# An attention and mixture-of-experts kernel: when one read is asked for, which engine squares 13 tiles, and where one counting and one router product stand

## The chip, the cores and the metric

The kernel runs on one core of a Trainium2 chip. The metric is the device time of one execution in microseconds; the time of a kernel is the median of its runs. The engines are called by their usual names: TensorE (PE in the profile; PEld is its weight load), VectorE (DVE), ScalarE (ACT), GpSimd (POOL) and SyncE (SP), which issues most of the DMAs.

## What is computed

Eight batches of 1856 tokens go through an attention without softmax; its output, token by token, goes through 16 experts in 4 groups, one expert for each token.

```python
scores = z @ z.T / S                  # z: 8 x 1856 x 64
out = u * (maximum(scores, 0)**2 @ v) # u, v: 8 x 1856 x 256
g = argmax(x @ w_group)               # x: the 14848 rows of out
e = argmax(x @ w_expert[g])
y[token] = softmax_g * softmax_e * (maximum(x @ w1[g, e], 0) @ w2[g, e])   # F = 1024
```

All is float32. The kernel splits each factor of a product into a high part and a low part and adds two or three products.

## The kernel before

**Attention.** A batch has 1856 queries, cut into four quarters (chunks) c = 0 to 3 of 512, 512, 512 and 320 columns in batches 1 to 7 (the last quarter is the one of 320), and 512, 512, 416, 416 in batch 0. Each quarter runs over 15 key tiles of 128 keys; one (batch, quarter, key tile) is a step s, and its place in the quarter is i. The order of the key tiles in a quarter stands in `KORD`. The main loop runs over the steps: `scores(s + 6)` prepares a step six ahead, `attn_v(s)` adds its products with v to the two banks o of the quarter.

**A native tile.** `scores` makes two score products into one of three score banks (lines 438 and 439), ScalarE reads the bank with Relu into r (L442), squares it, and from the square come a high part ah and a low part al. Two ways: ScalarE squares r in place (L450), VectorE copies it into ah (L451) and subtracts (L455, or L458 for the last key tile); or, in the tiles that `ACT_TWICE` lists by quarter, ScalarE squares twice, once into ah (L447) and once in place (L448), and VectorE only subtracts.

**A mirrored tile.** The score matrix is symmetric, so in batches 1 to 7 the tiles below the diagonal aren't computed again. VectorE transposes a tile in 32 x 32 blocks (st, mt), SP writes it to DRAM (sym), and later reads it back (at, `load_mirror`); ScalarE copies at into ah (L427), VectorE subtracts (L428). In the first three quarters the block on the diagonal is halved too: of its four key tiles the first two are transposed (dt), written by one DMA (dg, L362), and read back by four DMAs into dl (`load_diag`, L372); for the third and the fourth key tile only the right half is computed, and ScalarE copies the left half from dl (L466), VectorE subtracts (L467). `DGL` says how many steps before its first user the read is asked for, counted in `scores`.

**The end of a quarter.** `chunk_end` multiplies o by u into xT (VectorE, L508). Some steps later, by `defer`: xh (ScalarE, L514) and xl (VectorE, L519), `logits` (four router products pl, lines 561 and 562), `logits_out` (a copy lgp by ScalarE, L569, and a transposing DMA into lgx), and `planes` (copies by ScalarE, L543, and transposing DMAs that put the rows in order, L549). `LG` is the number of steps from the end of the quarter to `logits`; `logits_out` follows one step later, the planes begin at LG + 2 except in the third quarter.

**Routing.** `route(b, half, hs)` takes two quarters' logits (one, in the last half of batch 7), picks the expert in small VectorE operations, and counts: three products pk (L684 to L686) give each token its place in its expert's bucket, VectorE adds them to the running `base` (L700), and POOL scatters the rows to DRAM (L721). It is a generator, and the main loop takes two of its pieces in each step (three to five in batch 7). Before pk it yields a number: so many steps pass. pl and pk use the same single bank, ps_m.

**What sets the order.** From step 15 to the last quarter the order of TensorE, ScalarE and VectorE is the order of the code. The order on SP and POOL is made by a planner, which takes what the code emits first among what its own timing says is ready. Tiles r, ah, al, z, mt, dt and dl share 27 slots.

**Experts.** At the end of batch 6 the experts are sorted by their counts so far, the first expert's weights (raw_e) are loaded in batch 7 (its ScalarE copies are L204 and L197), and from about 773 us on all time goes to the experts' products.

Of the kernel before, what the change touches and what calls it, by code (L numbers as in the profile page):

```python
# [29 lines left out]
def tile_glu_attn_moe(  # L30
# [12 lines left out]
    B, D, S = uT.shape  # L43
# [7 lines left out]
    NK = NKF + 1  # L51
# [18 lines left out]
    HT = 64  # L70
    NST = 2
    NQT = 27
    ACT_TWICE = ((1, 7, 8, 10, 9, 11), (5, 9, 12), (), ())
    HALF = 256
    DGL = 4
    KT = 4
    MC = 4
    KB = [0, 1, 2, 3]
# [44 lines left out]
    def bank(pl, tag, name):  # L123
        return pl.tile([P, 512], F32, tag=tag, name=name)
# [94 lines left out]
    def defer(step, fn):  # L219
        deferred.append((step, fn))  # L220
# [154 lines left out]
    def load_mirror(b, c, cc):  # L375

        if cc < NQ - 1:
            at = new_at(f"at_{b}_{c}_{cc}").rearrange("p (g x) -> p g x", x=2 * P)
            src = sym.pop((b, c, cc)).rearrange("(g r) (j x) -> j r g x", r=32, x=2 * P)
            for j in range(4):  # L380
                nc.sync.dma_start(at[j * 32:(j + 1) * 32], src[j])
            ats[(b, c, cc)] = at.rearrange("p g (h t x) -> p t h g x", h=2, t=KT)
            return
        g = QW[b][cc] // 32
        at = new_at(f"at_{b}_{c}_{cc}").rearrange("p (g x) -> p g x", x=P)
        src = sym.pop((b, c, cc))[0:g * 32, :].rearrange("(g r) (j x) -> j r g x", r=32, x=P)
        for j in range(4):
            nc.sync.dma_start(at[j * 32:(j + 1) * 32, 0:g, :], src[j])
        ats[(b, c, cc)] = at[:, 0:g, :].rearrange("p g (t x) -> p t g x", t=KT)
# [9 lines left out]
    def key(b, c, i):  # L399
        if (b, c) == (B - 1, NQ - 1):  # L400
            return (0, 1, 12, 2, 3, 14, 4, 5, 13, 6, 7, 8, 9, 10, 11)[i]
        return KORD[c][i] if MB[0] <= b < MB[1] else i

    NS = len(steps)
# [4 lines left out]
    def scores(s):  # L409
# [3 lines left out]
        for far in (ATL, 12):  # L413
            lb, lc, li = steps[min(s + far, NS - 1)]
            lk = key(lb, lc, li)
            if lk % KT == 0 and mirrored(lb, lc, lk) and ((lc, lk) == (3, 8) and lb < B - 1) == (far != ATL):
                load_mirror(lb, lk // KT, KB[lc])
        lb, lc, li = steps[min(s + DGL, NS - 1)]
        lk = key(lb, lc, li)
# [25 lines left out]
        mirror = MB[0] <= b < MB[1] and KB[c] < MC and k // KT < MC and c < POS[k // KT]  # L445
        if k in (ACT_TWICE[c] if MB[0] <= b < MB[1] else ()) and s >= NK:
            held(nc.scalar.activation(out=ah, in_=a, func=AF.Square))  # L447
# [50 lines left out]
    def chunk_end(s):  # L498
        b, c, k = steps[s]
# [16 lines left out]
        def rest_x():  # L516
            xh, xl = xhl
            for d in range(ND):
                nc.vector.tensor_sub(out=xl[:, d, 0:w], in0=xT[:, d, :], in1=f32(xh[:, d, 0:w]))  # L519
# [18 lines left out]
        def planes(d):  # L538

            for t0, t1, q in ((0, w // P, P), (w // P, nt, part)):  # L540
                if t1 > t0:
                    src = xT[:, d, t0 * P:t0 * P + (t1 - t0) * q].bitcast(U16)
                    nc.scalar.copy(  # L543
                        out=pl[:, t0:t1, 2 * d:2 * d + 2, 0:q],
                        in_=src.rearrange("p (t q h) -> p t h q", q=q, h=2),
                    )
            if d == ND - 1:
                for t in range(nt):
                    nc.sync.dma_start_transpose(  # L549
                        rows[:, t, 0:D].bitcast(U16).rearrange("p (g d) -> p g d", d=P),  # L550
                        pl[:, t].rearrange("p g q -> p (g q)"),
                    )
# [20 lines left out]
                lgx.rearrange("p t h l -> p (t h) l"), lgp[:, 0:nt].rearrange("p t h q -> p (t h q)")  # L573
            )

        LG = (7 if b == B - 1 and c < 2 else (11 if c == 2 else 8 if c == 0 else 7)) if s + 1 < NS - NK else 2
        XO = 2 if s + 1 < NS - NK else 0
        (split_x() if XO == 0 else defer(s + XO, split_x))
        (rest_x() if XO == 0 else defer(s + XO + 1, rest_x))
        PL = XO + 1 if not XO or c == 2 else LG + 2  # L580
        defer(s + PL, lambda: planes(0))
        defer(s + PL + 1, lambda: planes(1))
        defer(s + LG, logits)
        defer(s + LG + (1 if XO else 0), logits_out)
        wait = 5 if last else 12 if b == 0 and c < 2 else (17 if c == 1 and b < B - 1 else 15) if s + 1 < NS - NK else 8
        alone = b == B - 1 and c >= NQ - 2
        if c % 2 or alone:
            gens.append((max(s + wait, PFILL[-1] + 2), route(b, c // 2, (c % 2,) if alone else (0, 1))))
# [21 lines left out]
    def route(b, half, hs):  # L610
# [65 lines left out]
        if len(hs) > 1:  # L676
            nc.vector.tensor_add(out=pre[:, 4:8], in0=pre[:, 4:8], in1=pre[:, 3:4].to_broadcast([P, 4, NE]))
            yield
        yield {(B - 1, 1, 0): 5, (B - 1, 1, 1): 1, (B - 2, 1, 0): 7, (0, 1, 0): 11}.get((b, half, hs[0]), 9 if half or b == B - 1 else 7)
        pk = bank(ps_m, "m", f"pk_{name}")  # L680
        W = NT8 * NE
        ohf = oh16.rearrange("p i e -> p (i e)")
# [179 lines left out]
    def phase1(name, wt, x, W, between=None, stack=True):  # L862
        xh, xl = x
        hs = []
        for f in range(NF):
            ps = bank(ps_s, "s", f"ph_{name}_{f}") if f % 2 == 0 else bank(ps_o, "o", f"ph_{name}_{f}")
            fs = slice(f * P, (f + 1) * P)
            o = ps[:, 0:W]
            for d in range(ND):
                nc.tensor.matmul(o, wt["l"][d][:, fs], xh[:, d, 0:W], start=(d == 0), stop=False)  # L870
                nc.tensor.matmul(o, wt["h"][d][:, fs], xh[:, d, 0:W], start=False, stop=False)  # L871
                nc.tensor.matmul(o, wt["h"][d][:, fs], xl[:, d, 0:W], start=False, stop=(d == ND - 1))  # L872
            hh = new_z(f"hh_{name}_{f}")
            hl_ = new_z(f"hl_{name}_{f}")
            nc.scalar.activation(out=hh[:, 0:W], in_=o, func=AF.Relu)  # L875
            wf = W - HT if stack and half(W) else W
            los = [(hl_[:, 0:wf], 0, wf)]
            if wf < W:
                los.append((hh[:, W:W + HT], wf, W))
            for dst, c0, c1 in los:  # L880
                nc.vector.scalar_tensor_tensor(out=dst, in0=o[:, c0:c1], scalar=0.0, in1=f32(hh[:, c0:c1]),  # L881
                                               op0=ALU.max, op1=ALU.subtract)
            hs.append((hh, hl_))
            if between:
                between(f)
        return hs
# [148 lines left out]
    for s in range(NS):  # L1035
        b, c, k = steps[s]
# [39 lines left out]
        if k == NK - 1:  # L1076
            chunk_end(s)
# [145 lines left out]
    for i, (e, r0, n) in enumerate(blocks):  # L1223
# [21 lines left out]
        hs = phase1(i, wts[e], x, n, mid, not turned)  # L1245
# [25 lines left out]
    with tc.If(kreg > 0) as _c, tc.For_i(0, kreg) as iv:  # L1271
# [18 lines left out]
        hs = phase1("ov", wt, x, OVT)  # L1290
# [42 lines left out]
```

## Time and profile before

| | us |
|---|---|
| median of 3 runs | 1464.62 (1464.35 to 1467.05) |
| the profiled execution | 1458.71 |
| its span, first to last instruction | 1457.0 |
| VectorE busy, share of the span | 79% |
| ScalarE busy, share of the span | 65% |

TensorE's clock was granted in full over the whole span (0.999 in the mean). The share of busy time is a mean over the attention part, where TensorE, VectorE and ScalarE all have much to do and the DMA engines as well, and the expert part, where TensorE alone is full. A wait is shown as an idle time of an engine and what ended it. The span's start is 0 us in all rows.

### The profile page before, as it was taken

How to read it: one execution, taken by the hardware profiler on the slowest of the kernel's cores; microseconds unless marked ns; L12 is line 12 of the kernel's file. 1: busy time of each engine (PE TensorE's matmuls, PEld its weight loads, DVE VectorE, ACT ScalarE, POOL GpSimd, SP SyncE). 2: the span in 40 equal slices, each digit the busy share in tenths (PEclk: the TensorE clock that was granted, in tenths of full speed). 3: DMA queues.
4: the chain of work that ended last, by engine and by line, in shares of the span. 5: the costliest groups of instructions: out<-in, count | busy, mean ns of one | idle time of the engine just before them, and what ended most of it. 6: DMA issues, size and time to landing. Idle time of an engine off the chain costs nothing. (4 is left out here: it accounts for less than half of the span.)

```text
span 1457.0 us, 22526 instructions
## 1 busy us (share of the span) xinstructions
PE 1434.2 (98%) x7113; PEld 1234.2 (85%) x7113; DVE 1144.1 (79%) x2388; ACT 940.3 (65%) x1690; POOL 322.5 (22%) x405
## 2 busy tenths in 40 slices
PE   9999999999999999999999999999999999999997
PEld 7888788878888888888878999898888888999986
DVE  7888989899998999989988576776565666566664
ACT  8888698797887988878865345444444444444442
POOL 0002033221332223212224222112111211222122
PEclk9999999999999999999999999999999999999999
DMA  9987979969799698997885464455434555555421
GB/s 320 334 220 214 243 176 266 245 188 245 186 271 245 181 244 196 260 241 181 222 215 154 102 168 98 118 131 137 127 82 118 136 125 132 128 138 133 129 61 44
DMA packets 394346, 260.61 MB, mean 179 GB/s; under 512 B 263424, under 2 KB 357508, under 8 KB 394225
## 3 DMA queue, kind: packets, MB, share of 16 engines
q1 hardware_dynamic: 382400, 228.13, 61.5%
q0 software_dynamic: 11744, 30.90, 7.3%
q8 instruction: 56, 0.92, 0.3%
q14 instruction: 66, 0.53, 0.1%
q10 hardware_dynamic: 80, 0.13, 0.0%
HBM read 113.79 MB, written 94.72 MB: 143 GB/s over the span
## 5 line engine op out<-in xcount | busy, mean ns | idle before, releaser
L486 PE MATMUL o<-ah,vl 128*128 128x512 f32 (+2 forms) x960 | 356.7, 372 | 7.0 <-DVE ah L451 4.2
L487 PE MATMUL o<-ah,vh 128*128 128x512 f32 (+2 forms) x960 | 354.6, 370 | 0.0
L489 PE MATMUL o<-al,vh 128*128 128x512 f32 (+2 forms) x896 | 330.6, 370 | 1.0 <-DVE al L428 0.8
L881 DVE SCALAR_TENSOR_TENSOR hl<-ph,hh 128x512 fp32r<-128x512 f32 (+12 forms) x288 | 174.0, 610 | 147.2 <-ACT hh L875 146.6
L944 PE MATMUL yT<-hh,w_e 128*128 128x512 f32 (+12 forms) x1120 | 268.8, 360 | 0.0
L875 ACT ACTIVATE hh<-ph 128x512 fp32r<-128x512 f32 (+12 forms) x288 | 153.6, 536 | 148.6 <-PE ph L872 146.0
L969 POOL DMA_INDIRECT out_dram<-y,meta x126 | 127.2, 1010 | 495.7 <-DVE y L967 476.1
L944 PEld LDWEIGHTS yT<-hh,w_e 128*128 128x128 f32 x1120 | 200.1, 188 | 25.2
L486 PEld LDWEIGHTS o<-ah,vl 128*128 128x128 f32 x960 | 180.2, 188 | 39.6 <-DVE ah L451 6.7
L871 PE MATMUL ph<-xh_m,w1h_e 128*128 128x512 f32 (+12 forms) x576 | 207.2, 360 | 0.0
L870 PE MATMUL ph<-xh_m,w1l_e 128*128 128x512 f32 (+12 forms) x576 | 206.8, 360 | 0.0
L442 ACT ACTIVATE r<-sc 128x512 f32<-128x512 f32 (+3 forms) x312 | 169.1, 542 | 58.3 <-PE sc L439 56.2
L872 PE MATMUL ph<-xl_m,w1h_e 128*128 128x512 f32 (+12 forms) x576 | 203.0, 359 | 0.0
L487 PEld LDWEIGHTS o<-ah,vh 128*128 128x128 f32 x960 | 180.3, 188 | 26.5
L489 PEld LDWEIGHTS o<-al,vh 128*128 128x128 f32 x896 | 168.1, 188 | 29.5 <-DVE al L455 2.3
L455 DVE TENSOR_TENSOR al<-r,ah 128x512 fp32r<-128x512 f32 (+3 forms) x280 | 177.1, 633 | 19.5 <-ACT r L448 2.6
L721 POOL DMA_INDIRECT bucket<-rows,di x121 | 135.1, 1116 | 176.6 <-DVE rows L718 88.4
L944 PE MATMUL yT<-hl,w_e 128*128 128x512 f32 (+12 forms) x560 | 159.1, 360 | 0.0
L947 ACT COPY yp<-yT 128x1024 uint16<-128x1024 uint16 (+2 forms) x70 | 59.3, 848 | 144.4 <-PE yT L944 140.0
L450 ACT ACTIVATE r<-r 128x512 f32<-128x512 f32 (+3 forms) x249 | 142.8, 573 | 7.9
L870 PEld LDWEIGHTS ph<-xh_m,w1l_e 128*128 128x128 f32 x576 | 108.2, 188 | 13.3
L871 PEld LDWEIGHTS ph<-xh_m,w1h_e 128*128 128x128 f32 x576 | 108.2, 188 | 13.0
(170 smaller groups left out, 2097.6 us busy)
## 6 DMA issues: line engine op xcount, KB each, us to landing
raw_e<-in_w_dram SPq DMA_DIRECT2D x64, 512.0 KB
sym<-st SPq DMA_DIRECT2D x42, 512.0 KB
at<-sym SPq DMA_DIRECT2D x84, 256.0 KB
bucket<-padrow SPq DMA_DIRECT2D x32, 660.0 KB
at<-sym SPq DMA_DIRECT2D x84, 160.0 KB
vr<-in_v_dram SPq DMA_DIRECT2D x23, 512.0 KB
ut<-in_uT_dram SPq DMA_DIRECT2D x23, 512.0 KB
sym<-mt SPq DMA_DIRECT2D x42, 256.0 KB
```

Source lines behind the costliest of these rows:

```text
L442: held(nc.scalar.activation(out=a, in_=ps[:, w0:w], func=AF.Relu, scale=1.0 / S))
L450: held(nc.scalar.activation(out=a, in_=a, func=AF.Square))
L455: held(nc.vector.tensor_sub(out=al, in0=a, in1=f32(ah)))
L486: held(nc.tensor.matmul(o, vl[:, dsl], ah, start=(i == 0), stop=False))
L487: held(nc.tensor.matmul(o, vh[:, dsl], ah, start=False, stop=end and al is None))
L489: held(nc.tensor.matmul(o, vh[:, dsl], al, start=False, stop=end))
L870: nc.tensor.matmul(o, wt["l"][d][:, fs], xh[:, d, 0:W], start=(d == 0), stop=False)
L871: nc.tensor.matmul(o, wt["h"][d][:, fs], xh[:, d, 0:W], start=False, stop=False)
L872: nc.tensor.matmul(o, wt["h"][d][:, fs], xl[:, d, 0:W], start=False, stop=(d == ND - 1))
L875: nc.scalar.activation(out=hh[:, 0:W], in_=o, func=AF.Relu)
L881: nc.vector.scalar_tensor_tensor(out=dst, in0=o[:, c0:c1], scalar=0.0, in1=f32(hh[:, c0:c1]), op0=ALU.max, op1=ALU.subtract)
L944: nc.tensor.matmul(o, wt["2"][f // 2][:, w0:w0 + P], hs[f][q // 2][:, 0:n], start=((f, q) == (0, 0)), stop=((f, q) == (NF - 1, 2)))
```

## The change

The change moves work, and neither adds nor removes a product. `DGL` goes from 4 to 7. `ACT_TWICE`, by quarter, goes from six and three key tiles to eight and five. `LG` of batch 7's second quarter (c = 1) goes from 7 to 9; that of its first quarter stays 7. The counting products of `route(0, 0)` come 10 steps after the yield ahead of them, and not 7; those of `route(0, 1)` lose their entry (11) and fall to the 9 of all second halves.

```diff
-    ACT_TWICE = ((1, 7, 8, 10, 9, 11), (5, 9, 12), (), ())
+    ACT_TWICE = ((0, 4, 1, 6, 5, 8, 10, 11), (5, 10, 9, 11, 12), (), ())
...
-    DGL = 4
+    DGL = 7
...
-        LG = (7 if b == B - 1 and c < 2 else (11 if c == 2 else 8 if c == 0 else 7)) if s + 1 < NS - NK else 2
+        LG = (7 + 2 * c if b == B - 1 and c < 2 else (11 if c == 2 else 8 if c == 0 else 7)) if s + 1 < NS - NK else 2
...
-        yield {(B - 1, 1, 0): 5, (B - 1, 1, 1): 1, (B - 2, 1, 0): 7, (0, 1, 0): 11}.get((b, half, hs[0]), 9 if half or b == B - 1 else 7)
+        yield {(B - 1, 1, 0): 5, (B - 1, 1, 1): 1, (B - 2, 1, 0): 7, (0, 0, 0): 10}.get((b, half, hs[0]), 9 if half or b == B - 1 else 7)
```

## Rows read from the trace of the kernel before

**Rows 1.** The page, first part: engine, busy us (share of the span) xinstructions.

```profile
PE 1434.2 (98%) x7113; PEld 1234.2 (85%) x7113; DVE 1144.1 (79%) x2388; ACT 940.3 (65%) x1690; POOL 322.5 (22%) x405
```

**Rows 2.** TensorE's waits, whole span: tile and line <- releaser: total us, times, longest.

```profile
PE o L486 <- DVE ah L451: 4.2, 5, 1.1
PE o L486 <- DVE ah L458: 2.6, 5, 0.5
PE pl L561 <- DVE base L700: 2.2, 1, 2.2
PE pk L684 <- ACT lgp L569: 1.7, 1, 1.7
PE pl L562 <- DVE xl L519: 1.6, 1, 1.6
```

**Rows 3.** Stretches, fourth quarters (batches 1 to 6): length, busy of PE, PEld, DVE, ACT, POOL.

```profile
655.04:675.39 20.35, 18.64 (x114) 16.60 (x113) 19.54 (x46) 18.30 (x36) 6.57 (x9) 1.00 0.65 135
sum 117.53, PE 111.45 PEld 99.69 DVE 113.27 ACT 105.07 POOL 39.32; mean PE 18.57 PEld 16.62 DVE 18.88 ACT 17.51 POOL 6.55
```

**Rows 4.** TensorE in time, batch 6: start, us, line, operation [idle before <-releaser].

```profile
665.29 0.41 PE L486 MATMUL o<-ah,vl 128*128 128x320 f32 x1 [1.12 <-DVE ah L451]
...
666.29 0.31 PE L487 MATMUL o<-ah,vh 128*128 128x320 f32 x1
666.44 0.31 PE L489 MATMUL o<-al,vh 128*128 128x320 f32 x1
```

**Rows 5.** ScalarE's waits, 110 to 770 us; ScalarE in time, third quarters.

```profile
ACT ah L466 <- DMA dl<-dg: 23.0, 16, 3.8
...
182.60 0.41 ACT L466 CAST ah<-dl 128x256 fp32r<-128x256 f32 x1 [2.41 <-DMA dl<-dg]
...
644.23 0.39 ACT L442 ACTIVATE r<-sc 128x256 f32<-128x256 f32 x1 [1.44 <-PE sc L439]
...
647.58 0.41 ACT L466 CAST ah<-dl 128x256 fp32r<-128x256 f32 x1 [2.52 <-DMA dl<-dg]
```

**Rows 6.** VectorE in time, end of batch 6's third quarter and behind it.

```profile
649.66 0.30 DVE L451 CAST ah<-r 128x256 fp32r<-128x256 f32 x1 [1.21 <-ACT r L450]
...
651.85 1.23 DVE L293 TENSOR_TENSOR vl<-vr,vh 128x1024 fp32r<-128x1024 f32 x1 [1.10 <-ACT vh L292]
...
659.32 1.28 DVE L508 TENSOR_TENSOR xT<-o,ut 128x512 f32<-128x512 f32 x2
```

**Rows 7.** SP's DMA issues in time, batch 6's third quarter.

```profile
633.26 4.64 SPq L549 DMA_TRANSPOSE rows<-pl  x3
...
639.58 0.44 SPq L495 DMA_DIRECT2D ut<-in_uT_dram  x1
640.11 0.54 SPq L372 DMA_DIRECT2D dl<-dg  x1
...
641.79 1.63 SPq L372 DMA_DIRECT2D dl<-dg  x3
```

**Rows 8.** SP's waits, 110 to 770 us, at the issue of dl.

```profile
SPq L372 <- DMA dg<-dt: 11.2, 5, 3.3
```

**Rows 9.** ScalarE and TensorE in time, start of batch 6's first quarter.

```profile
576.74 0.63 ACT L447 ACTIVATE ah<-r 128x512 fp32r<-128x512 f32 x1
577.40 0.63 ACT L448 ACTIVATE r<-r 128x512 f32<-128x512 f32 x1
...
578.84 0.59 ACT L442 ACTIVATE r<-sc 128x512 f32<-128x512 f32 x1
...
580.95 0.48 PE L438 MATMUL sc<-zm,z2h 128*128 128x512 f32 x1
```

**Rows 10.** ScalarE in time, batch 7's third quarter.

```profile
741.10 1.00 ACT L569 COPY lgp<-pl 48x1024 uint16<-48x1024 uint16 x1
...
743.03 1.04 ACT L543 COPY pl<-xT 128x1024 uint16<-128x1024 uint16 x1
747.57 1.15 ACT L204 CAST w_e<-raw_e 128x512 fp32r<-128x512 f32 x2 [3.50 <-DMA raw_e<-in_w_dram]
```

## The prediction

> **What bounds the kernel now.** I read the page's first part, then TensorE's waits, then the stretches in which it waits. TensorE is busy 1434.2 us of the 1457.0 us span [rows 1], so no more than 22.8 us can be won without taking products away, and the change takes none away. TensorE's five longest waits for other engines sum to 12.3 us [rows 2], and all are at lines of the attention part. The expert part behind it shows none of that size, so a wait taken out of attention shortens the span one for one, if it doesn't come back later.
>
> The waits are of two kinds. Three stand once each: the first counting product pk waits 1.7 us for the copy lgp (batch 0), a router product pl waits 2.2 us for `base` (batch 1), another waits 1.6 us for xl (batch 7) [rows 2]. The rest, "o waits for ah", stands mostly in the fourth quarter (c = 3) of batches 1 to 6. Six such quarters last 117.53 us together, 20.35 the one of batch 6 [rows 3]. There the first wait is 1.12 us; TensorE's products of 320 columns start 0.15 us apart and are drawn 0.31 us long [rows 4], so an idle time begins 0.16 us behind the moment at which the next product could have started. With that, the quarter's two waits (1.12, and 0.54 for the ah of L458) and the products right behind them, which start about 0.1 us late five times, come to 2.5 us, and the quarter without them to 17.85 us. 117.53 - 6 x 17.85 = 10.4 us is lost in these six.
>
> Why: in the third quarter ScalarE, in order, reaches the copy of the diagonal's transposed quarter (L466) and waits for its read dl: 2.52 us in batch 6, from 645.06 to 647.58 [rows 5]; the six idle times in the third quarters of batches 1 to 6 (the first, 2.41 us, and the last are shown) sum to 10.6 us; ScalarE's waits for dl in all quarters are 23.0 us [rows 5]. VectorE then waits 1.21 us for ScalarE's r and 1.10 us for vh [rows 6], and after that has no gap until the late ah. It reaches xT at 659.32 [rows 6], though TensorE began the fourth quarter at 655.04 [rows 3]. So VectorE enters the fourth quarter 4 us late, and what it is late there TensorE pays. The six waits for dl (10.6) and the six losses (10.4) are nearly the same sum.
>
> **Part 1, the read asked for seven steps ahead.** The order of ScalarE, VectorE and TensorE is fixed by the code, and the read moves on SP's queue alone. In the third quarter it is now emitted at step i = 3, behind the u read of that step; with 7 it is emitted at i = 0, ahead of u but still behind the transposes of rows and the z read (emitted at i = 11 and 12 of the quarter before). In batch 6 SP issues rows from 633.26 to 637.9, then z and two mirror writes, u at 639.58, one dl at 640.11, then v and a mirror write, then three dl from 641.79 [rows 7]. Ahead of u the four stand from 639.58: the first 0.53 us earlier, the other three from 640.1 instead of 641.79, 1.7 us earlier, and they overtake three transfers of 256 to 512 KB besides. Taken at 2.0 us: of the wait of 2.52, 0.5 stays. In the six batches I take min(wait, 2.0): 2.0 + 1.5 + 1.1 + 2.0 + 1.0 + 2.0 = 9.6. VectorE can follow that far, because its gaps just there (1.21 + 1.10) are larger, and it doesn't run into TensorE's end of the quarter, of which it is 4 us late. **Sum -9.6 us.** Bounds: nothing at all (the read lands as late as now) to -10.4. I take the value near the upper end because the issue order, [rows 7], leaves little else to hold it. What is late next: ScalarE's vh, z2h and `at` copies behind it show no wait in that stretch of the trace, so they move up with it. Queued behind the four dl on SP are u, v and the mirror writes, 2 us later at most; ScalarE and VectorE show no wait for u or v anywhere in batches 1 to 6. In the first two quarters nothing is won on TensorE, which doesn't wait there; in the second the dl already stands on SP waiting for its own write to land (11.2 us in 5 waits, [rows 8]), and an earlier issue only makes SP stand longer.
>
> **Part 2, ScalarE squares twice in 13 tiles for 9.** In the first quarter 0, 4, 6, 5 are added and 7, 9 taken out, in the second 10, 11 are added. Each added tile takes a copy (L451; 0.30 us for 256 columns at 649.66 [rows 6], so up to 0.6 for 512) from VectorE and gives ScalarE a second square, 0.66 us from the start of L447 to the start of L448 [rows 9]. TensorE shows no wait for VectorE in these quarters of batches 1 to 6, so that gain is worth nothing there. ScalarE's cost may not: the next score product but two needs a score bank that L442 frees. In batch 6 the product of tile 8 starts at 580.95 and the bank that it takes was freed by tile 6's L442 (578.84 + 0.59 = 579.43): 1.52 us of room [rows 9]. Tiles 0 and 4 stand before it and add 2 x 0.66 = 1.32, which leaves 0.2; the tiles up to 5 have the same order of room. So TensorE waits between 0 (room enough) and 0.66 us (one square on the path) in each of six batches: 0 to +4 us; I take 0.1 each, near the row's room. **Sum +0.6 us.**
> The Trainium skill's "ScalarE: Activation LUTs", section "What ACT_TABLE_LOAD costs", gives an ACTIVATE with immediate operands 186 ns + 0.833 ns an element, with 93 ns of overlap back to back: by estimate 0.52 us for 512. The trace has 0.66. By the page's figure the two squares would leave 0.5 us of room and this part would cost nothing.
>
> **Part 3, the countings.** The first counting (0, 0) comes three steps later, at the last step of batch 0. lgp has long been copied then, so the wait of 1.7 us (1.84 with the pitch) goes. Its VectorE steps and eight scattering DMAs on POOL come three steps later too; the next user of its bank is five steps behind. The counting (0, 1) loses its entry and comes after 9 steps, not 11: `base` two steps earlier, five and not three steps before the router product that waits 2.2 us (2.39) for it. VectorE is that much ahead of TensorE or the scores themselves would wait. What is late next is xl for the same product, emitted between, so I leave 0.5. **Sum -1.8 - 1.9 = -3.7 us.** Bounds: -4.2, and 0 if VectorE's lag turns up as waits in batch 1.
>
> **Part 4, the router product of batch 7's second quarter two steps later.** The wait for xl (1.6, with pitch 1.76) goes. But lgp, the planes and their transposes move by two steps too, and that puts them behind a wait: lgp (741.10, 1.00 us) and the first planes copy (743.03, 1.04 us) now run while ScalarE has nothing better, before it waits 3.50 us for the weights until 747.57 [rows 10]. Moved, these 2.04 us come behind 747.57, among tiles that TensorE needs at once. So about what is won is paid back in the fourth quarter: between -1.8 and +2. **Sum 0.**
>
> **Sum.** -9.6 + 0.6 - 3.7 + 0 = -12.7. The profiled execution took 1458.71 us (span 1457.0) and would take 1446.0. The median of the runs, 1464.62, stands 5.9 above it; nothing here explains the difference, so I carry it: 1464.62 - 12.7 = 1451.9.
>
> **Rivals.**
> (a) The read lands no earlier, as the DMA engines and not SP's order set its landing, or VectorE's own load in the fourth quarter takes the place of the wait. For it: the last dl is issued by 643.4 and its user starts at 647.58 [rows 5, 7], so 4 us of the way are in the engines. Against: what it now waits behind there is just what it would overtake. Then of part 1 no more survives than what the first dl gains, 0.53, in six batches: 0 to -3.2, taken as -2, and the time is 1464.62 - 2 + 0.6 - 3.7 = 1459.5.
> (b) Hardly any gain: ScalarE becomes the bound at the start of the first quarter. If the whole square (0.66) stands on the path twice in each of six batches, +7.9, and 1464.62 - 9.6 + 7.9 - 3.7 = 1459.2; with half of part 1 failing as well, 1464.0.
> (c) Slower: SP blocks. If the planner puts the early read ahead of the row transposes and the z read, SP must stand until dg has landed. From 633.26 that could be up to 639.6: dg is issued just before 633.26 and dl at 640.11 went without a wait, so the write landed by then. z is then read up to 6 us later, and ScalarE, which already waits for z there, has 1.44 us of waiting for scores and the 2.52 us for dl [rows 5] to give; 6 - 4 = 2 us of lateness stay and go to the fourth quarter, on top of its loss. 6 x 2 + 0.6 - 3.7 = +8.9: 1473.5. It decides from about 4 us of blocking. For it: SP does wait for dg in second quarters [rows 8]. Against: rows and z are emitted earlier than the read and are ready.
> The Trainium skill's "DMA: Bandwidth & Descriptors", section "Anatomy of one DMA", has it that a semaphore wait of a DMA happens on the issuing sequencer, before dispatch. By that rule the early read would hold the queue as in (c); the trace agrees with 11.2 us of SP waiting for dg.
>
> **How the numbers follow.** Forecast 0.62, (a) 0.15, (b) 0.13, (c) 0.10. The forecast's own range runs from everything won, 1464.62 - 10.4 - 4.2 - 1.8 = 1448, to 1457 with half of part 1. The range over the cases runs from 1447.5 to 1463, beyond which lie (c) and a part of (b). About 0.2%, 2.9 us, is what a measurement of this kernel can tell from no change: the forecast and most of (a) and (b) are faster, 0.78; within 0.12; slower 0.10, which is (c).
>
> **What would show it.** Right: ScalarE's wait before L466 in third quarters under 0.6 us; VectorE's xT within 2.5 us of TensorE's end of that quarter; fourth quarters of 17.9 to 18.4 us; no wait of pk for lgp in batch 0. Wrong: score products (L438) that wait for ScalarE's r in first quarters; z2h waiting over 3 us; batch 7's fourth quarter longer than before by over 3.

## The result

The change made the kernel **slower**: 1476.66 us median (1474.71 to 1481.13) against 1464.74 for the kernel before in the same comparison, a ratio of 1.0082 with a 95% interval of 1.0056 to 1.0109. That is 12 us lost where 12.7 were forecast to be won, and outside the range. The profiled execution took 1481.13 us, its span 1479.4. That is the slowest of the four, and the profiled execution of before (1458.71) is among the fastest of all its runs (1458 to 1469), so the two traces lie 22.4 us apart and not 12: the sums read from them below show where time goes and not how much of the 12 us it is.

The page's first part of the kernel after: VectorE has 11 us less work than in [rows 1], ScalarE 11 us more, as the second squares intend. TensorE is busy 13 us longer with the same 7113 instructions. Some 2.5 us of the two traces' difference lie in the expert part, from its first product to the end (695.1 us for 692.6); more of this under the countings.

```profile
PE 1447.1 (98%) x7113; PEld 1237.9 (84%) x7113; DVE 1132.7 (77%) x2360; ACT 951.6 (64%) x1718; POOL 321.4 (22%) x405
```

TensorE's waits over the whole span, after. The wait of pk for lgp of [rows 2] is not among them; the router product pl now waits for `base` four times and for xl five times, where it waited once for each.

```profile
PE pl L561 <- DVE base L700: 5.2, 4, 1.5
PE o L486 <- DVE ah L451: 4.5, 6, 1.7
PE o L489 <- DVE al L428: 3.5, 6, 0.8
PE pl L562 <- DVE xl L519: 3.4, 5, 0.7
```

These waits stand in another place than before. The fourth quarters of batches 1 to 6, where the gain was to come from, last 117.08 us for 117.53 in [rows 3]: in sum nothing won, nothing lost. Two of the six (batches 4 and 6) did come to 17.86 us, as forecast; those of batches 1 and 2 last 21.2. The third quarters lost 19 us. First their sum in the kernel before, then one of them (batch 4) and the sum after; the columns are length, then busy time of PE, PEld, DVE, ACT and POOL, the granted TensorE clock, DMA share and GB/s.

```profile
sum 136.26, PE 134.03 PEld 109.26 DVE 116.17 ACT 90.89 POOL 30.64; mean PE 22.34 PEld 18.21 DVE 19.36 ACT 15.15 POOL 5.11
```

```profile
454.28:481.70 27.42, 24.49 (x104) 18.73 (x102) 21.06 (x46) 17.89 (x34) 5.41 (x5) 0.94 1.05 244
...
sum 155.22, PE 143.23 PEld 111.99 DVE 120.15 ACT 95.91 POOL 32.16; mean PE 23.87 PEld 18.66 DVE 20.03 ACT 15.98 POOL 5.36
```

In the kernel before, five of the six last 22.28 us each, without a gap. After, batch 4's lasts 27.42. Of the 19 us, 10 are idle (155.22 - 143.23 for 136.26 - 134.03) and 9 are busy time with the same products. In four of the six the granted clock is 0.94, which by the estimate at the end of this text makes some 5 of the 9; the rest was not taken apart.

What ScalarE waits for in batches 1 to 6 (after). Its waits for dl, 20.6 us in this stretch before, are down to 2.1, as forecast, and in third quarters of batches 1 to 6 there is none. But 22.8 us of waiting for mirror writes (sym <- mt) are new, and its waits for z went from 5.2 to 12.2.

```profile
ACT xh L514 <- DVE xT L508: 33.4, 11, 5.8
ACT r L442 <- DMA sym<-mt: 22.8, 8, 3.5
ACT r L442 <- PE sc L439: 16.4, 14, 1.8
ACT z2h L247 <- DMA zr<-in_zT_dram: 12.2, 9, 4.4
...
ACT ah L466 <- DMA dl<-dg: 2.1, 3, 1.0
```

VectorE's waits in batches 2 to 6, after. The waits for mirror writes (12.4 + 7.0) were 0.9 before, and the list of before has none for ScalarE's second square (L448) in these batches.

```profile
DVE al L455 <- DMA sym<-mt: 12.4, 6, 3.1
DVE al L455 <- ACT r L448: 12.1, 12, 1.7
DVE ah L451 <- DMA sym<-mt: 7.0, 5, 2.0
DVE z2l L254 <- ACT z2h L247: 5.3, 5, 1.9
```

Why does a tile of r, ah or al wait for a *write* of another tile? r, ah, al, z, mt, dt and dl share 27 slots. A new tile may be written only when its slot's last holder is done with, and an mt tile is done with when its write to DRAM has landed. The waits show who stands for mt's slots: before, some ah of VectorE (0.9 us in batches 2 to 6) and no tile of ScalarE; after, ah and al of VectorE and, in the first quarter of each of batches 1 to 6, an r of ScalarE (3.1 to 3.5 us). Who takes such a slot without standing for it, no trace shows.

And why is the write late? SP in time, batch 2's first quarter; before, then after (the columns are start, time at the queue, the issue, and how many).

```profile
210.22 0.38 SPq L362 DMA_DIRECT2D dg<-dt  x1
211.88 3.18 SPq L325 DMA_DIRECT2D sym<-st  x2
...
217.67 0.32 SPq L381 DMA_DIRECT2D at<-sym  x1
218.09 1.38 SPq L372 DMA_DIRECT2D dl<-dg  x3
219.52 0.45 SPq L342 DMA_DIRECT2D sym<-mt  x1
```

```profile
207.85 0.53 SPq L362 DMA_DIRECT2D dg<-dt  x1
209.74 0.34 SPq L325 DMA_DIRECT2D sym<-st  x1
210.18 2.31 SPq L372 DMA_DIRECT2D dl<-dg  x4
...
216.24 1.80 SPq L381 DMA_DIRECT2D at<-sym  x4
218.14 0.39 SPq L342 DMA_DIRECT2D sym<-mt  x1
```

The early read stands right behind the write it depends on, with one st write between. All four at reads then come ahead of mt's write; before, one did. The write is issued hardly later, 10.3 us behind dg for 9.3. But it lands later: by the semaphores' updates in the traces, in batches 2 to 6 it takes 6.2 to 6.6 us from issue to landing, where it took 2.7 to 4.5. ScalarE pays for it; the write issued at 218.14 lands at 224.71:

```profile
224.79 0.60 ACT L442 ACTIVATE r<-sc 128x512 f32<-128x512 f32 x1 [3.43 <-DMA sym<-mt]
```

SP's standing for dg before it can issue dl has grown too, over 110 to 770 us from the 11.2 of [rows 8] to 31.1. But it isn't what makes this write late. Of the 31.1 us, 27.0 stand in the second quarters of batches 2 to 6, 4.9 to 5.8 us in each (0.7 to 3.3 before), the rest in batch 7; in no first quarter does SP stand for dg.

```profile
SPq L372 <- DMA dg<-dt: 31.1, 7, 5.8
```

### The profile page after: what moved, and what is told of

Its sections match the earlier page's. It is cut to its first block, busy times and chain, and to the rows that moved or that the text cites. A ratio compares the mean times of both kernels' runs of the same rounds, so it can differ in the third digit from the quotient of the medians.

```text
span 1479.4 us, 22522 instructions
## 1 busy us (share of the span) xinstructions
PE 1447.1 (98%) x7113; PEld 1237.9 (84%) x7113; DVE 1132.7 (77%) x2360; ACT 951.6 (64%) x1718; POOL 321.4 (22%) x405
## 4 chain that ended last, share of the span: by engine, by line
PE 66%; DVE 6%; issue 3%; DMA 3%; ACT 1%; POOL 1%; SPq 1%; DVEq 0%; POOLq 0%; ACTq 0%
PE yT L944 21%; PE ph L870 7%; PE ph L871 7%; PE ph L872 7%; PE o L486 6%; PE o L487 6%; PE o L489 5%; PE sc L438 2%; PE sc L439 2%; DMA sym<-mt 1%; DVE al L428 1%; PE pl L562 1%; DVE xT L508 1%; DVE mt L334 1%; DVE al L455 1%
## 5 line engine op out<-in xcount | busy, mean ns | idle before, releaser
L870 PE MATMUL ph<-xh_m,w1l_e 128*128 128x512 f32 (+12 forms) x576 | 207.6, 362 | 0.0
L487 PEld LDWEIGHTS o<-ah,vh 128*128 128x128 f32 x960 | 181.4, 189 | 26.9
L450 ACT ACTIVATE r<-r 128x512 f32<-128x512 f32 (+3 forms) x221 | 125.1, 566 | 7.0
L870 PEld LDWEIGHTS ph<-xh_m,w1l_e 128*128 128x128 f32 x576 | 108.2, 188 | 13.9
L872 PEld LDWEIGHTS ph<-xl_m,w1h_e 128*128 128x128 f32 x576 | 107.9, 188 | 14.2
```

The costliest lines, as they stand in the source:

```text
L487: held(nc.tensor.matmul(o, vh[:, dsl], ah, start=False, stop=end and al is None))
```

## The experiments

All times are medians, the ratio is that to the kernel before in the same comparison, with its 95% interval. "Stretch" is the time from the start of batch 2 to that of batch 7 in the profiled execution; "V mt", "S mt" and "S z" are VectorE's and ScalarE's waits for mirror writes, and ScalarE's for z, in that stretch.

| kernel | us | ratio (interval) | stretch | V mt | S mt | S z |
|---|---|---|---|---|---|---|
| before | | 1 | 465.2 | 0.9 | 0 | 6.3 |
| after | 1476.66 | 1.0082 (1.0056, 1.0109) | 485.0 | 19.4 | 19.8 | 11.2 |
| e1 read at 7 | 1472.01 | 1.0056 (1.0037, 1.0075) | 482.1 | 12.6 | 22.6 | 15.4 |
| e2 second squares | 1466.82 | 1.0019 (1.0007, 1.0030) | 476.3 | 7.9 | 0 | 3.0 |
| e3 countings | 1462.22 | 0.9993 (0.9978, 1.0007) | 471.0 | 1.0 | 0.1 | 3.3 |
| e8 router product | 1463.86 | 1.0007 (0.9994, 1.0019) | 468.6 | 1.8 | 0 | 6.5 |
| e4 read at 7, third quarter | 1460.82 | 0.9989 (0.9976, 1.0002) | 468.1 | 8.3 | 0 | 15.3 |
| e5 read at 7, first two | 1475.87 | 1.0080 (1.0058, 1.0102) | 480.8 | 3.9 | 15.4 | 4.2 |
| e6 dl in its own slot | 1482.10 | 1.0114 (1.0085, 1.0144) | 487.2 | 13.8 | 19.4 | 15.4 |
| e7 e4, z early | 1454.44 | 0.9947 (0.9928, 0.9967) | 461.6 | 11.1 | 0 | 4.5 |
| e10 z early alone | 1467.40 | 1.0033 (1.0020, 1.0046) | 474.2 | 1.9 | 0 | 4.2 |
| e9 e5, mt's write first | 1468.81 | 1.0047 (1.0033, 1.0061) | 475.8 | 10.7 | 0.9 | 2.4 |
| e11 all quarters, both mended | 1460.71 | 0.9985 (0.9973, 0.9998) | 473.3 | 24.0 | 0.4 | 3.1 |
| e13 e11, mt in own slots | 1456.68 | 0.9951 (0.9937, 0.9965) | 464.6 | 1.0 | 0 | 16.0 |
| e14 e7, mt in own slots | 1452.67 | 0.9927 (0.9914, 0.9940) | 457.9 | 0 | 0 | 9.3 |
| e15 the change, both mended | 1471.37 | 1.0053 (1.0035, 1.0071) | 476.5 | 26.9 | 0.3 | 2.9 |
| e12 e7 with the countings | 1456.93 | 0.9965 (0.9954, 0.9975) | 462.1 | 9.6 | 0 | 3.3 |
| e16 e14 with the countings | 1453.42 | 0.9930 (0.9915, 0.9944) | 459.9 | 0 | 0 | 6.9 |

The stretches are set against each other and not only against the 465.2 of before.

**One part at a time.** The two theories: S, the early read, through slots and SP's queue; T, the second squares, which put ScalarE behind.

```diff
-    DGL = 4
+    DGL = 7
```

> The kernel before with the read asked for seven steps ahead, and nothing else of the change. Theory S (the early read takes a slot of the 27 of tag q three steps sooner, so that another tile gets the slot that a mirror tile mt holds until its write has landed, and SP stands before the read): most of the loss is here. The countings are worth about -3.7 us, so this kernel comes to 1464.7 + 11.9 + 3.7 = about 1480, at least 1473; its trace has ScalarE waits of 3 us for sym<-mt at L442 once in each first quarter of batches 1 to 6, and third quarters in which TensorE waits 4 to 5 us. Theory T (the second squares put ScalarE behind, and all its copies and SP's transposes come late after it): this kernel gains what was forecast for part 1, or at least loses nothing: 1455 to 1465.

```diff
-    ACT_TWICE = ((1, 7, 8, 10, 9, 11), (5, 9, 12), (), ())
+    ACT_TWICE = ((0, 4, 1, 6, 5, 8, 10, 11), (5, 10, 9, 11, 12), (), ())
```

> The kernel before with the 13 tiles per batch that ScalarE squares twice, and nothing else of the change. Theory S: as in the forecast, 0 to +4 us: 1464.7 to 1468.7, without waits of L442 for sym<-mt in first quarters. Theory T: most of the loss is here, 1473 to 1480, with TensorE waits of 4 to 5 us in third quarters as after the whole change.

```diff
-        yield {..., (0, 1, 0): 11}.get(
+        yield {..., (0, 0, 0): 10}.get(
```

> The kernel before with the two countings moved, and nothing else of the change. Both theories: -3.7 us by the forecast (-4.2 to 0): 1461.0. The waits of pk for lgp in batch 0 and of pl for base in batch 1 are gone.

```diff
-        LG = (7 if b == B - 1 and c < 2
+        LG = (7 + 2 * c if b == B - 1 and c < 2
```

> The kernel before with only the router product of batch 7's second quarter two steps later. Forecast 0 (-1.8 to +2): 1463. The changed kernel's last fourth quarter had 5.46 us of stalls for 1.99 before, with ScalarE waiting 6.9 us for raw_e for 3.5. If the product's move alone does that, this kernel is 2 to 4 us slower, 1465 to 1467, and its batch 7 shows both numbers; if not, these come from elsewhere in the change, and batch 7 is as before.

The read alone loses 0.56%, 8 us, and shows the waits of the whole change (V mt 12.6, S mt 22.6); T can't give that. The second squares cost 0.19%, 3 us, the countings, forecast at 3.7 us of gain, and the router product nothing that can be told from zero. Together +11 us of the 12. Theory S missed its figure for e1 (1473 at least): it had given the read what the other parts took.

VectorE's waits in e2, batches 2 to 6, show what the second squares do. VectorE saves 8 us of copies in the stretch (busy 429 for 437 us) and waits 12.4 us for the second square itself, which stands behind the first on ScalarE.

```profile
DVE al L455 <- ACT r L448: 12.4, 12, 1.7
```

Batch 7 of e8: ScalarE's wait for the weights is longer by 1.6 us (3.5 in [rows 10]), and the fourth quarter lasts 24.77 us where it lasted 21.36, while the third is 1.0 shorter. So what the router product wins is paid back there, and this part alone brings most of the long last quarter that the whole change shows.

```profile
ACT w_e L204 <- DMA raw_e<-in_w_dram: 5.1, 1, 5.1
```

**Which quarter.** `DGL` becomes one number for each of the three quarters.

```diff
-    DGL = 4
+    DGL = (4, 4, 7)    # e4; (7, 7, 4) in e5
```

> The kernel before with the read seven steps ahead in the third quarter alone, four in the first two. Theory S has two forms. S1 (what hurts is who gets mt's slot in first quarters, the ScalarE tile of step 13): here first and second quarters are as before and the third gains: 1455 to 1460. S2 (what hurts is in the third quarter itself, SP standing before the read with z, mt and u behind it, or VectorE's tiles getting mt's slots there): slower, 1470 to 1478, with TensorE waits of 4 us in third quarters, and none of L442 for sym<-mt in first quarters. Theory T says 1455 to 1465 as for the read in all quarters.

> The read seven steps ahead in the first and second quarter, four in the third; nothing else of the change. The read in all quarters cost 0.56% and in the third alone gained 0.1%. Theory S1 (the loss comes from the first two quarters: there r of step 13 gets the slot of a mirror tile whose write stands on SP behind four reads of at, and ScalarE waits 3.4 to 4.8 us): here +0.5 to +0.7%, 1470 to 1473, with that wait in each first quarter. Rival I (neither alone costs, but the two together, as ScalarE and VectorE come late into a third quarter that has no room left): here within 0.2% of the kernel before, 1460 to 1466, with the L442 wait for sym<-mt there and no stall of TensorE behind it in third quarters.

The loss is in the first two quarters: 0.80%, with r's wait in each first quarter of batches 1 to 5 (3.2 to 4.5 us) and in batch 6 another of 3.3. The read in the third quarter doesn't hurt, but its gain of 9.6 us isn't there either. SP in e4, batch 6's third quarter, and ScalarE a little later:

```profile
640.40 1.51 SPq L372 DMA_DIRECT2D dl<-dg  x3
...
643.54 0.98 SPq L282 DMA_DIRECT2D vr<-in_v_dram  x2
...
645.17 2.09 SPq L388 DMA_DIRECT2D at<-sym  x3
647.36 0.41 SPq L242 DMA_DIRECT2D zr<-in_zT_dram  x1
```

```profile
655.58 0.62 ACT L247 CAST z2h<-zr 128x512 fp32r<-128x512 f32 x1 [3.41 <-DMA zr<-in_zT_dram]
```

Before, the same z read (the second quarter's of the next batch) went out right behind the last dl of [rows 7]:

```profile
643.54 0.38 SPq L242 DMA_DIRECT2D zr<-in_zT_dram  x1
```

Counted from the start of the quarter (632.76 before, 634.05 in e4), z moved back from 10.8 to 13.3 us, behind two v reads and three at reads. Why the planner puts z there is not shown; a slot of z's that comes free later by its reckoning would fit, but in e6 below, where dl is out of the pool, ScalarE waits as long for z (15.4 us). In e4 ScalarE waits for z (15.3 us) where it waited for dl.

**Slots or order.** dl gets a slot of its own, beside 27 for the rest.

```diff
-        at = new_zraw(f"dl_{b}_{c}")
+        at = sb("dl", [P, 512], F32, 1, f"dl_{b}_{c}")
```

> The read seven steps ahead in all quarters, as in e1_read7, but dl has a slot of its own and the other tiles of tag q keep 27; room for it comes from the unused pad, one of three y tiles, and the warm tile. SP's order around the first and third quarter's reads is that of e1_read7, with the read even a place earlier. Theory S (slots): r of step 13 no longer gets mt's slot, ScalarE's L442 waits for sym<-mt fall from 3.4 to 4.8 us to under 1, and the loss goes: 1455 to 1465. Theory Q (SP's order is what costs: what stands behind the early read comes late, mt's write, u, v and the second z): as e1_read7, 1469 to 1474.

Theory S in its slot form fell: by its median this is the slowest kernel of all. It is also 8 us above theory Q's figure, for which the runs show one reason in part: room for dl's slot was made by giving the y tiles of the routing and the expert part two slots instead of three. VectorE's waits for the writes of y go from some 20 us to 40, and the expert part takes 694.2 us for 692.6. e13, e14 and e16 below have the same two slots, and 1.5 to 2.2 us of the same loss. r no longer stands for mt's slot, but ScalarE's next writer, the ah of L447, does, and waits as long:

```profile
ACT ah L447 <- DMA sym<-mt: 19.4, 5, 4.9
```

Another tile gets that slot; what decides is when mt's write lands, and that goes by the order on SP, as e9 will show. Here too four at reads stand ahead of it, and it takes 6.5 to 8.1 us to land.

**Mending the order, third quarter.** z's read is asked for two steps earlier.

```diff
-        ("z", 1, (2, 4), (2, 11))
+        ("z", 1, (2, 2), (2, 11))
```

> As e4_read7_third (seven steps ahead in the third quarter alone), and the read of the second z quarter of the next batch is asked for two steps earlier, so that it stands on SP right behind u and ahead of v and at. In e4 that read was issued at 647.36 and landed at 655.5 in batch 6 (before: 643.54 and 647.9), and ScalarE's z2h waits for z took the place of its waits for dl (19.9 us in 11 for 6.4 in 5). Theory Z (the z read put behind the early dl ate the gain): the z waits go back under 8 us, and 3 to 7 us are gained against e4: 1453 to 1458. Rival V (VectorE's own work sets when the fourth quarter's tiles are ready): z waits go, the time stays as e4, 1459 to 1463, and VectorE has no idle time of over 1 us in third quarters.

> The kernel before (read four steps ahead) with only the read of the second z quarter asked for two steps earlier, as in e7. If e7's gain needs both moves (the read of the diagonal early, and z not behind it), ScalarE waits for dl in third quarters as before, and the time is within 0.2% of the kernel before: 1460 to 1465. If it came from z alone, 1453 to 1457.

z now goes out right behind u, 9.5 us into the quarter (639.55, the quarter begins at 630.03), and of the third quarters' waits for dl 0.5 us is left; ScalarE's waits for z fall from 15.3 to 4.5, and the time from 0.9989 to 0.9947 of before: what the forecast looked for in part 1 was there, once z was out of the way. Theory Z is borne out; the early z alone loses 0.33%, more than expected, as dl then stands behind z (waits for dl 23.1 us in the stretch, 13.1 before). Both moves are needed.

**Mending the order, first quarters.** The writes of mt and the at reads of the first quarter are held in the order of the code, mt first.

```diff
-        nc.sync.dma_start(sym[pair][kk * P:kk * P + h, :], t2[0:h])
+        (pin if c == 0 else same)(nc.sync.dma_start(sym[pair][kk * P:kk * P + h, :], t2[0:h]))
-                nc.sync.dma_start(at[j * 32:(j + 1) * 32], src[j])
+                (pin if c == 0 and cc == 1 else same)(nc.sync.dma_start(at[j * 32:(j + 1) * 32], src[j]))
```

> As e5_read7_first_two, and the writes of the mirror tiles mt of the first quarter and the reads of at that follow are held in the order in which the code asks for them, so that the write of mt 12 stands on SP ahead of the four at reads and not behind them, as it does in the kernel before (one at read ahead of it there). Theory Q1 (the early read pushes mt's write behind the at reads; it lands 3 us later, and whichever tile of ScalarE gets its slot waits for that): the L442 waits for sym<-mt in first quarters fall from 3.2 to 4.5 us to under 1.5, and at least half of the 13 us goes: 1462 to 1469. Rival R (SP itself is late, as it stands before the early read until dg has landed, and all that it issues behind that is late): the at reads and u are late all the same, and ScalarE waits for at or VectorE for u in place of mt: 1471 to 1477.

> The read seven steps ahead in all three quarters, mt's write held ahead of the at reads in first quarters, and the second z read two steps earlier: both of SP's orders mended. Theory Q1: within 0.3% of e7_third_z_early: 1453 to 1460. Rival R (SP standing before the read in first and second quarters costs by itself): 1464 to 1470, half of e5's loss and more on top of e7.

SP of e9, batch 2's first quarter: mt's write comes ahead of the at reads, it lands 2.3 to 2.7 us after its issue in batches 2 to 6, and ScalarE's waits for it are gone (15.4 to 0.9). The read still goes out right behind dg, 2.2 us later.

```profile
209.78 2.29 SPq L372 DMA_DIRECT2D dl<-dg  x4
...
216.37 0.33 SPq L342 DMA_DIRECT2D sym<-mt  x1
216.74 0.42 SPq L282 DMA_DIRECT2D vr<-in_v_dram  x1
217.27 0.94 SPq L381 DMA_DIRECT2D at<-sym  x2
```

About 0.33 of 0.80% went, within Q1's range at its upper end, though less than the half it asked for. SP still stands 26.9 us for dg, in second quarters; what the other 0.47% are (that standing, or VectorE's 10.7 us for mirror writes) no run separates. e11 lies between the two theories (0.9985): Q1 is not the whole of it.

**What was left.** In e11 VectorE waits 24.0 us for slots that mt holds. mt gets three slots of its own, 25 stay for the rest.

```diff
-    NQT = 27
+    NQT = 25
-        t2 = new_zraw(f"mt_{b}_{c}_{k}")
+        t2 = sb("mt", [P, 512], F32, 3, f"mt_{b}_{c}_{k}")
```

> As e11_all_quarters_mended (read seven steps ahead everywhere, mt's first-quarter write ahead of at, z early), and the mirror tiles mt have three slots of their own beside 25 for the rest, with room from the unused pad, one of three y tiles and the warm tile. SP's order is that of e11. Theory M (what is left of the loss is VectorE waiting for slots that mt holds until its write lands): VectorE's waits for sym<-mt in batches 2 to 6 fall from 24.0 us to under 6, and 8 to 15 us go: 1446 to 1454. Theory R (SP standing before the reads makes other transfers late): VectorE or ScalarE waits for something else that SP reads, and the time stays at 1458 to 1464.

> As e7_third_z_early, with the same three slots of their own for mt; SP's order is that of e7. If VectorE's idle time goes into the time one for one, its waits for sym<-mt (11.1 us in batches 2 to 6 of e7) fall to under 3 and 5 to 8 us are gained on e7: 1446 to 1450. If TensorE's own work bounds by now (its stalls in e7's batches 2 to 6 were 5.6 us), no more than 5.6 can be had: 1449 to 1454.

VectorE's waits in batches 2 to 6: e11, then e13.

```profile
DVE al L455 <- DMA sym<-mt: 19.5, 10, 3.7
DVE ah L451 <- DMA sym<-mt: 4.5, 5, 1.4
```

```profile
DVE mt L334 <- DMA sym<-mt: 1.0, 1, 1.0
```

With 23 us of VectorE's waiting gone, 0.34% (5 us) is won: theory M holds in direction and for some 60% of its least figure, not one for one. Another 2 us were won and lost again in the expert part, by the y tiles (694.7 us for 692.5). Waits for z (16.0 us) came in place of VectorE's. SP stands for dg as long as ever (30.1 us), so that standing alone costs hardly more than the 0.24% by which e13 lies above e14, which reads early in the third quarter alone. e14 won 3 us on e7, not 5 to 8: in its profiled execution the stretch of batches 2 to 6 is TensorE's own work but for 0.1 us, so nothing more was to be had there (columns as for the quarters above).

```profile
206.24:664.13 457.89, 457.79 (x2231) 384.69 (x2230) 436.42 (x972) 384.59 (x721) 120.19 (x150) 1.00 0.93 230
```

e14 is the fastest kernel: 0.73% below before, 1.5% below after. It holds one part of the change, the read at seven in the third quarter alone, with z early and slots for mt.

**The whole change, mended.**

> The whole change, with mt's first-quarter writes held ahead of the at reads and the second z read two steps earlier, as in e11. If the parts add up (e11 -1.7, second squares +2.8, countings -0.9, router product +1.0): 1462.4 + 1.2 = 1463.6, within 1460 to 1468. If the second squares do their harm only together with the early read (ScalarE later, and SP's transposes behind it): 1470 or more.

1471.37: the parts don't add up. On e11 the rest of the change, which alone costs 3 us, costs 10 (1.0053 for 0.9985), 2.5 of them in the expert part, where e15 takes 695.0 us. VectorE waits 10.6 us for second squares and 26.9 for mt's slots; whether the squares do that through ScalarE or through yet another deal of slots was not taken apart.

**The countings, twice more.**

> e7_third_z_early with the two countings moved as in the change. e3 put these at -0.07% of the kernel before; what TensorE wins there was given back in the attention part behind it. If VectorE sets the pace of batches 1 to 6 whatever TensorE does, the countings win nothing here too: 1453 to 1455. If TensorE's waits add one for one, 3.7 us less than e7: 1450.7.

> e14_third_z_mt_own (0.9927 of the kernel before) with the two countings moved as in the change. In e14's profile TensorE still stands 2.24 us in the last quarter of batch 0, and 0.64 in the third of batch 1. In e3 the first stood at 1.0 and the second at 0.2. If TensorE sets the pace of what follows, 1.2 + 0.4 = 1.6 us are won: 0.9916, and batch 1's first quarter begins 1.2 to 2 us earlier with batch 7's as much earlier. If not, the lead shrinks on the way: batch 7 begins where it did in e14 (664.1), 0.9927.

Neither gains, and e12 lies above both of its figures. The reason stands outside the attention part, among the experts. From its first product ph (L870) to the end of the span, it takes 692.2 to 692.6 us in before and in each of the nine kernels that have neither the countings nor the y tiles changed. With the countings it takes 695.1 (after), 695.3 (e3), 695.5 (e12) and 695.0 (e15); with two y slots 694.1 (e14), with both 696.9 (e16). So the countings make it some 2.8 us longer each time. The products of L870 in e7, then in e12; behind the colon stand shortest, median and longest in ns, then the first and the last start in us, then the shapes:

```profile
L870 PE MATMUL ph<-xh_m,w1l_e x576: 276/386/482, 760.0 to 1436.9; 128*128 128x512 f32 x92, 128*128 128x256 f32 x15, 128*128 128x320 f32 x11, 128*128 128x336 f32 x11
```

```profile
L870 PE MATMUL ph<-xh_m,w1l_e x576: 277/384/477, 759.6 to 1439.3; 128*128 128x512 f32 x92, 128*128 128x256 f32 x15, 128*128 128x320 f32 x11, 128*128 128x336 f32 x11
```

The same 576 products begin 0.4 us earlier and end 2.4 later. The difference grows little by little over all experts, and the traces show no longer idle time of TensorE there; why is open. Ahead of the experts the countings did win something: taking the 2.8 us off the differences of the ratios leaves, by estimate, 3.8 us in e3, 0.2 in e12 and 2.4 in e16, each within some 2 us.

## Why the prediction was wrong

**What bounds.** Right in its rows, and incomplete. dl did hold ScalarE, VectorE and then TensorE; e7 and e14, which take the third quarters' waits for it away (10.6 us, 2.1 of which the trace of before puts down to the z read; 0.5 in e7, 1.8 in e14) and keep z in place, win 8 and 11 us. But the view was of waits as they stood, and none of the 27 slots was looked at. A slot is a resource like a queue, and the rows of before do show it: VectorE waits for mirror writes there too, 0.9 us in batches 2 to 6.

**Part 1 (-9.6; measured +8).** Two of its sentences fell.
- "What is late next" was answered by the engines that showed no wait. It listed u, v and the mirror writes as queued behind the four reads, "2 us later at most", and looked for waits for u and v only. The second z read stood behind them too, it moved 2.5 us in e4, and its user had no room. And a mirror write that is late isn't waited for under its own name: it holds a slot.
- "In the first two quarters nothing is won ... an earlier issue only makes SP stand longer" was right about the standing, and the two quarters were priced at nothing. They were the largest term: e5 has +0.80% for them alone. It should have been asked what takes the places that the read leaves on the queue: in the first quarter the four at reads, ahead of mt's write, which then lands 6.2 to 6.6 us after its issue for 2.7 to 4.5. e9, which puts the write first, gets 0.33 of the 0.80% back.

The gain itself was sized well: the dl waits went as forecast, and e7, with z out of the way, shows 0.53%, 8 us for the forecast 9.6.

**Rival (c)**, with 0.10, gave 1473.5 for a measured 1476.66, and that is luck: its mechanism is not what was measured. SP does stand longer for the early read, 31.1 us for 11.2. But in the third quarters of batches 1 to 6, where (c) put its price, it does not stand for it: rows and the first z read go out ahead (in batch 6 z at 656.24, the read from 657.34 on), as the argument against (c) said. It stands in second quarters, and e13 stands there as long and is 0.49% faster than before. What cost was the order behind the read: the second z, and in first quarters the at reads ahead of mt's write. The Trainium skill's rule cited there ("DMA: Bandwidth & Descriptors", section "Anatomy of one DMA", a DMA's semaphore wait is served on the issuing sequencer) agrees with both traces (11.2 and 31.1 us).

**Part 2 (+0.6, bounds 0 to 4; measured +2.8).** Inside its bounds alone, by another way. In e2's batches 2 to 6 TensorE shows no wait of a score product for a bank (in the kernel after there is one, 0.7 us in batch 0). VectorE, which the part took to be ahead, stands for the second square, 12.4 us in e2, more than the 8 us of copies it saves. "That gain is worth nothing there" held for TensorE; the loss on VectorE wasn't looked for. Rival (b) thus named the right engine and the right place (the longest of these waits, 1.3 to 1.7 us, stand at the starts of first quarters), and the wrong waiter.

**Part 3 (-3.7; measured -1 with 0 inside its interval).** The waits go as said: after, pk waits no longer, and batch 1 begins at 111.65 in e3 for 114.08 before. The sum took the expert part as given, and that step failed: with the countings moved it is some 2.8 us longer, in all five kernels that have them, and that eats the gain or most of it. How much was won ahead of the experts, 0.2 to 3.8 us by the estimate above, doesn't decide between the forecast and the case of VectorE's lag, which it put at 0.

**Part 4 (0).** Right: +0.07%, 0 inside its interval, and paid back in batch 7's fourth quarter as described.

**The signs.** "Right" came for ScalarE's L466 in third quarters, for pk, and for two of the six fourth quarters; "wrong" for z2h (4.4 us, over 3) and for batch 7's last quarter (25.1 us for 21.4). That both kinds came shows which part they belonged to: the waits named were gone, and the time was elsewhere.

## What to carry to other kernels

When a transfer is asked for earlier, write down everything on its queue between the old place and the new, and for each who uses it *and which buffer it sets free*; a write that lands late is a wait of whoever gets the buffer, under another name. Where a pool of slots is shared by tiles of several engines, any move can deal the slots out anew: find out whose slot each new tile takes before a time is forecast. And set the parts that a change does not touch beside each other too, kernel by kernel: here the expert part held to within 0.4 us in ten kernels, and 2.8 us in it hid behind a part that seemed to win nothing.

## What the runs showed of the hardware

TensorE's granted clock was 1.00 through almost all of the kernel before. In the kernel after it fell to about half, which is the lower of its two levels (1.2 of 2.4 GHz), in four short stretches, each inside a third quarter, behind its waits (batches 2, 4, 5 and 6), besides its last few us, where before has the same. In batch 2:

```profile
268.00:273.00 5.00, 2.32 (x9) 1.04 (x7) 4.90 (x12) 3.75 (x7) 0.00 (x0) 1.00 0.79 170
273.00:276.50 3.50, 3.26 (x9) 2.38 (x10) 3.38 (x11) 2.04 (x6) 0.00 (x0) 0.54 0.85 272
276.50:281.00 4.50, 4.50 (x21) 3.70 (x21) 3.01 (x8) 4.47 (x8) 3.42 (x4) 0.98 1.08 308
```

TensorE had been busy 2.32 of 5 us; then 9 products took 3.26 us, and at full clock 21 took 4.50. At that pace the 9 would have needed 1.9, so by estimate such a stretch costs about 1.3 us, and the four some 5 of the 20 us by which batches 2 to 6 are longer. These waits of TensorE were thus paid a second time, in the products that followed them.
